# More and smaller products without use in TensorE's early gaps, on an attention and MoE kernel

## The chip, the cores and the metric

The kernel runs on one core of a Trainium2 chip. The metric is the device time of one execution in microseconds (us). Three runs of the kernel before gave 218.28, 218.58 and 218.94 us; their median is 218.58 us. "PE" is TensorE's matmul stream, "PEld" its weight loads, "DVE" VectorE, "ACT" ScalarE, "POOL" GpSimd (which here issues the input transfers) and "SP" SyncE (which issues the stores and the transposing transfers).

## The reference

Inputs are q, k and v of shape (4 batches, 8 heads, 768 positions, 64 channels) and two weights, 512x2048 and 2048x512. In each head every query sees the keys that are less than 16 positions away, and beside them 24 summaries, one for each block of 32 positions: the maximum of the block's keys and the mean of its values.

```python
k_sum = k.reshape(B, H, nb, block, D).max(axis=3)
v_sum = v.reshape(B, H, nb, block, D).mean(axis=3)
# local scores inside the window, and block scores + log(32), in one softmax
a = softmax(concat([where(mask_l, scores_l, -1e9), scores_s + log(block)]))
x = (a @ concat([v, v_sum])).transpose(0, 2, 1, 3).reshape(B * S, H * D)
h = x @ w_in
out = (h * clip(h + 3.0, 0.0, 6.0) / 6.0) @ w_out
```

The attention gives 3072 rows of 512 values, and two dense products with a gate between them make the output of 3072x512 float32.

## The kernel before, in words

Everything is recorded first and issued later. Each piece of work is registered with `plan.op(engine, cost, function, reads, writes, ...)` under a key such as `u03.0`: a letter for the kind, the batch, a number, and after the point the place among the pieces of that kind. The long string ORDER at the top lists all keys in the order in which the planner takes them. `Plan.run` (L141 ff.) gives every piece a begin and an end by fixed costs, gives PSUM banks and buffers to it, and sorts the pieces by begin; each engine then gets its instructions in that order. The planner's times fix nothing but the order and the choice of buffers; on the chip each engine works through its own list and waits on semaphores.

TensorE's pieces near the change are, for batch 0:

- `k0p.0` (`k_step`, L509): 16 transposes of 64x96 blocks of the keys of head pair p into an `h` bank.
- `q0p0.0` (`q_step`, L548): 8 such transposes for the queries.
- `s0p0.0` (`scores`, L629): two products of the identity with a table of large negative numbers, which lay the mask into a score bank; `s0p0.1` (L641) adds the scores themselves, 12 products.
- `u0p.0` (`vsum_first`, L665): 12 products that sum the values by blocks, for head pair p.
- `v00`, `v01`, `v02` (`values` and `finish`, L742 to L746, L775, L779, L797): the weighted sums of the values for 128 rows, their scaling on DVE into a tile `xn`, and four transposes of that by TensorE (L797).
- `q0p1.0` (`q_rest`, L561): three transposes of the rest of the queries.
- `F00...` (`f1`, L815): the first dense product, in parts of 128 columns for the first three groups of features; L820 (ACT) and L822 (DVE) make the gate, and L835 (`f2`) is the second dense product. Pieces `F` and `G` of earlier halves of batches fill TensorE between the attention steps of later ones.
- `u1.0`, `u2.0`, `u3.0` (`vsum`, L682): the sums by blocks for batches 1 to 3, 48 products each. They need every load of that batch's values, among them the short rows that `load_halo` brings (L467, L470).

Input transfers are issued by POOL in ORDER's order: `load_v` (L445), `load_halo` (L467, L470), `load_nat` (L424, L425), `load_raw` (L434), weights (L479, L485). A later transfer on POOL's queue reuses the semaphore of one eight transfers back or so, and waits for its landing.

What the change touches is the last piece of the kernel function. When the order is known, a loop goes over TensorE's pieces in their order and looks at the gap that the planner left ahead of each, up to the planner's time `WARM`. In such a gap it puts products without use: the tile `idle` (all ones) times itself, into a bank that the planner does not use at that time. Before the planner's time SLOW (5.8 us) one product of 512 columns is counted as 0.43, after it as 0.22, with 0.15 of the gap left free:

```python
n = int(max(min(o.begin, SLOW) - end, 0.0) / 0.43 + max(o.begin - 0.15 - max(end, SLOW), 0.0) / 0.22) + (end == BEGIN["PE"])
```

No result reads what these products write, but each one stands in TensorE's list, with a weight load of its own (both at L927), and what follows it on TensorE comes after it.

Of the kernel before, what the change touches and what calls it, by code (L numbers as in the profile page):

```python
# [84 lines left out]
SLOW = 5.8  # L85
# [3 lines left out]
BEGIN = {"PE": 1.6, "ACT": 0.8, "DVE": 0.9, "POOL": 1.4, "SP": 1.0}  # L89
# [138 lines left out]
def kernel(  # L228
# [9 lines left out]
    nc = tc.nc  # L238
    B, H, S, _ = q.shape
# [7 lines left out]
    NTILE = B * 2  # L247
    HQ = NQ // 2
    NS = S // 128
    WARM = 23.0  # L250
    EITHER = ("ACT", "DVE")
    ENGINE = {"DVE": nc.vector, "POOL": nc.gpsimd}
    ET = mybir.EngineType
# [7 lines left out]
    def sb(shape, dt, name):  # L261
        return const.tile(shape, dt, tag=name, name=name)
# [22 lines left out]
    idle = sb([128, 512], BF16, "idle")  # L285
# [635 lines left out]

    def keep(n, o):
        o = o[:, 0] if any(o is x for x in pairs) else o[:]
        for _ in range(n):
            nc.tensor.matmul(o, idle[:, 0:128], idle[:], start=True, stop=True)  # L927

    order = plan.run()
    banks = [s for p in BANKS for _, s in plan.pools[p]]  # L930
    todo, end = [], BEGIN["PE"]
    for o in order:
        if o.eng == "PE" and o.begin < WARM:
            n = int(max(min(o.begin, SLOW) - end, 0.0) / 0.43 + max(o.begin - 0.15 - max(end, SLOW), 0.0) / 0.22) + (end == BEGIN["PE"])
            idle_ = [s for s in banks if not any(a < o.begin and z > end and x is s for a, z, x in plan.lives)]
            if n > 0 and idle_:
                todo.append(lambda n=n, s=idle_[-1]: keep(n, s))
            end = max(end, o.end)
        todo.append(o.fn)
    for fn in todo:  # L940
# [29 lines left out]
```

## Time and profile before

| | |
|---|---|
| runs of the kernel | 218.28, 218.58, 218.94 us, median 218.58 |
| the profiled execution's own time | 219.68 us |
| its span in the profile | 217.9 us, 1.78 us less than its own time |
| PE busy | 207.1 us, 95% of the span |
| DVE, ACT, POOL busy | 148.3, 122.3 and 71.2 us |
| products without use | 19 weight loads of the tile `idle`; 16 of their matmuls are recorded |

The profiled execution is 1.10 us above the median of the three runs. Times in the trace are counted from the start of the span. A row of the timeline merges instructions of one kind that follow each other: start, time from the first start to the last end, engine, line, what is written from what, shapes, count, and in brackets how long the engine stood idle before it and what ended that. Ends of matmuls are modelled and contain the way through the array, so consecutive rows overlap; starts are what one compares. A few matmul records are missing.

### The profile page before, as it was taken

How to read it: one execution, taken by the hardware profiler on the slowest of the kernel's cores; microseconds unless marked ns; L12 is line 12 of the kernel's file. 1: busy time of each engine (PE TensorE's matmuls, PEld its weight loads, DVE VectorE, ACT ScalarE, POOL GpSimd, SP SyncE). 2: the span in 40 equal slices, each digit the busy share in tenths (PEclk: the TensorE clock that was granted, in tenths of full speed). 3: DMA queues.
4: the chain of work that ended last, by engine and by line, in shares of the span. 5: the costliest groups of instructions: out<-in, count | busy, mean ns of one | idle time of the engine just before them, and what ended most of it. 6: DMA issues, size and time to landing. Idle time of an engine off the chain costs nothing.

```text
span 217.9 us, 5201 instructions
## 1 busy us (share of the span) xinstructions
PE 207.1 (95%) x2125; PEld 118.4 (54%) x2151; DVE 148.3 (68%) x304; ACT 122.3 (56%) x236; POOL 71.2 (33%) x90
## 2 busy tenths in 40 slices
PE   7888999999989999989999999999999999999993
PEld 2566666765545555555555555555555555555552
DVE  4878998794898999849987866695555456333301
ACT  5697967797762545777742688833436343423010
POOL 7999369810988466296000000000000000000000
PEclk9999999999999999999999999999999999999999
DMA  5999999999999999999927920005421001201213
GB/s 68 182 156 191 201 164 159 205 195 147 122 120 164 169 122 143 162 172 148 212 52 180 230 26 0 3 0 157 135 48 51 0 2 50 99 0 48 86 59 100
DMA packets 109929, 24.67 MB, mean 113 GB/s; under 512 B 101072, under 2 KB 106960, under 8 KB 109904
## 3 DMA queue, kind: packets, MB, share of 16 engines
q0 software_dynamic: 93440, 14.89, 110.3%
q1 hardware_dynamic: 16464, 9.44, 16.4%
q8 instruction: 17, 0.28, 0.5%
q14 instruction: 8, 0.07, 0.1%
HBM read 29.77 MB, written 6.29 MB: 165 GB/s over the span
## 4 chain that ended last, share of the span: by engine, by line
PE 53%; DMA 25%; POOL 17%; issue 3%; ACT 0%; POOLq 0%; ACTq 0%
PE h L815 23%; PE o L835 22%; DMA vaug<-in_v_dram 20%; DMA win<-in_moe_w_in_dram 5%; PE h L835 5%; POOL nat L434 4%; POOL vaug L445 3%; POOL nat L425 2%; PE S L742 2%; POOL wout L485 1%; PE S L641 1%; POOL qwide L412 1%; POOL win L479 1%; POOL nat L392 1%; POOL nat L399 1%
## 5 line engine op out<-in xcount | busy, mean ns | idle before, releaser
L822 DVE SCALAR_TENSOR_TENSOR g<-r,h 128x384 bf16<-128x384 f32 x128 | 67.8, 547 | 42.6 <-ACT r L820 41.3
L815 PE MATMUL h<-x,win 128*128 128x384 bf16 (+1 forms) x536 | 94.5, 319 | 0.0
L820 ACT ACTIVATE r<-h 128x384 f32<-128x384 f32 x128 | 60.4, 496 | 55.2 <-PE h L815 51.6
L835 PE MATMUL o<-wout,g 128*128 128x512 bf16 x313 | 78.4, 379 | 1.6 <-issue 0.6
L815 PEld LDWEIGHTS <-win 128*128 128x128 bf16 x536 | 49.3, 98 | 34.0 <-issue 0.2
L835 PEld LDWEIGHTS <-g 128*128 128x128 bf16 x400 | 38.2, 98 | 37.2
L651 ACT ACTIVATE at<-S 120x768 bf16<-120x768 f32 x32 | 25.2, 816 | 4.7 <-PE S L641 4.6
L445 POOL DMA_DIRECT2D vaug<-in_v_dram x16 | 15.4, 968 | 4.4 <-DMA wout<-in_moe_w_out_dram 2.3
L655 DVE TENSOR_TENSOR at<-at,mask 96x768 bf16<-96x768 bf16 x28 | 14.7, 550 | 1.7 <-ACT at L651 1.6
L494 ACT COPY ot<-o 128x512 f32<-128x512 f32 x14 | 8.3, 589 | 13.3 <-PE o L835 13.2
L779 DVE TENSOR_TENSOR xn<-S,rc 128x512 bf16<-128x512 f32 x23 | 15.4, 683 | 0.3
L425 POOL DMA_DIRECT2D nat<-in_k_dram x12 | 10.7, 898 | 4.4 <-DMA win<-in_moe_w_in_dram 3.3
L425 POOL DMA_DIRECT2D nat<-in_q_dram x12 | 10.6, 897 | 1.9 <-DMA win<-in_moe_w_in_dram 1.9
L835 PE MATMUL h<-wout,g 128*128 128x256 bf16 (+1 forms) x64 | 10.7, 326 | 0.1
L707 DVE TENSOR_REDUCE red<-kb 128x48 bf16<-128x1536 bf16 x6 | 10.5, 1745 | 0.0
L641 PEld LDWEIGHTS <-kb 64*128 64x128 bf16 x384 | 6.8, 95 | 6.2 <-issue 5.0
L742 PEld LDWEIGHTS <-at 120*64 120x64 bf16 x360 | 6.7, 111 | 4.9 <-issue 2.9
L742 PE MATMUL S<-vaug,at 120*64 120x65 bf16 x352 | 8.0, 197 | 0.9 <-DVE vaug L494 0.9
L494 ACT COPY vaug<-vs 24x768 bf16<-24x768 bf16 x9 | 7.4, 828 | 1.1 <-DVE vs L494 0.9
L494 DVE COPY vaug<-vs 24x768 bf16<-24x768 bf16 x15 | 7.7, 517 | 0.5
L494 ACT COPY ot<-h 128x256 f32<-128x256 f32 (+1 forms) x3 | 1.3, 443 | 11.6 <-PE h L835 11.6
L494 DVE COPY ot<-o 128x512 f32<-128x512 f32 x7 | 4.8, 688 | 4.4 <-PE o L835 2.6
(107 smaller groups left out, 155.8 us busy)
## 6 DMA issues: line engine op xcount, KB each, us to landing
out_dram<-ot SPq DMA_DIRECT2D x19, 256.0 KB, 2.5
vaug<-in_v_dram POOLq DMA_DIRECT2D x16, 192.0 KB, 9.6
win<-in_moe_w_in_dram POOLq DMA_DIRECT2D x4, 512.0 KB, 9.4
wout<-in_moe_w_out_dram POOLq DMA_DIRECT2D x4, 512.0 KB, 10.0
nat<-in_k_dram POOLq DMA_DIRECT2D x12, 128.0 KB, 8.4
nat<-in_q_dram POOLq DMA_DIRECT2D x10, 128.0 KB, 5.4
nat<-in_k_dram POOLq DMA_DIRECT2D x6, 192.0 KB, 6.7
nat<-in_q_dram POOLq DMA_DIRECT2D x6, 192.0 KB, 10.7
```

Of the source, the lines that this page charges most:

```text
L425: nc.gpsimd.dma_start(out=o[n:128], in_=src[b, :, lo + n:lo + 128].rearrange("h r d -> r h d"))
L445: op("POOL", 0.945, lambda: nc.gpsimd.dma_start(out=o[BLK:WIN, lo:hi, 0:D], in_=rows[:, lo:hi]), w=[("v", b % 2, c)], dma=1.28, els=1536)
L494: {"ACT": nc.scalar.copy, "DVE": nc.vector.tensor_copy, "POOL": nc.gpsimd.tensor_copy}[eng](o, i)
L651: op("ACT", 0.81, lambda a=a, x=x: nc.scalar.activation(a, x.slot[0:KEYS, :, 0:HALF], AF.Exp, scale=scl), r=[x], w=[("at", p, half)])
L655: op("DVE", 0.55, lambda m=m, half=half: nc.vector.tensor_tensor(m, m, mask[:, low(half):low(half) + HQ].unsqueeze(1).to_broadcast([WIN, 2 ...
L707: nc.vector.tensor_reduce(red.slot[:].rearrange("x (p u e n) -> x e u p n", p=NP, u=NS, e=2)[:, e], w[:, n * e:n * e + n, BLK:WIN].rearran ...
L742: nc.tensor.matmul(y, a[:, cols], vaug[b % 2][0:KEYS, h, t, 0:D + 1], start=True, stop=True)
L779: nc.vector.tensor_tensor(o, src[..., 0:D], r.unsqueeze(len(r.shape)).to_broadcast(list(o.shape)), op=ALU.mult)
L815: nc.tensor.matmul(h.slot[:, lo * 128:hi * 128], w_in_sb[:, kt, ft * 128:(ft + 1) * 128], xt[s].slot[:, kt, lo * 128:hi * 128], start=(kt ...
L820: op("ACT", 0.49, lambda: nc.scalar.activation(r.slot[:], h.slot[:, 0:HALF], AF.Relu, bias=0.5, scale=1.0 / 6.0), r=[h], w=[r], alloc=r)
L822: op("DVE", 0.553, lambda: nc.vector.scalar_tensor_tensor(gt[s].slot[:, ft], r.slot[:], 1.0, h.slot[:, 0:HALF], op0=ALU.min, op1=ALU.mult) ...
L835: nc.tensor.matmul(o.slot[:, a:z], gt[s].slot[:, ft, ts * 128:(ts + 1) * 128], w_out_sb[:, ft, a:z], start=(ft == 0), stop=(ft == NFT - 1))
```

## The change

The time up to which gaps are looked at, `WARM`, goes from 23.0 to 28.0. Past SLOW, 0.06 of the gap is left free and no longer 0.15, and a 512-column product is counted as 0.2158. What remains of the gap is filled with products of 128 columns (counted as 0.056 each). The part of a gap that lies before SLOW is treated as it was.

```diff
-    WARM = 23.0
+    WARM = 28.0
...
-    def keep(n, o):
+    def keep(n, m, o):
         o = o[:, 0] if any(o is x for x in pairs) else o[:]
-        for _ in range(n):
-            nc.tensor.matmul(o, idle[:, 0:128], idle[:], start=True, stop=True)
+        for c in [512] * n + [128] * m:
+            nc.tensor.matmul(o[:, 0:c], idle[:, 0:128], idle[:, 0:c], start=True, stop=True)
...
         if o.eng == "PE" and o.begin < WARM:
-            n = int(max(min(o.begin, SLOW) - end, 0.0) / 0.43 + max(o.begin - 0.15 - max(end, SLOW), 0.0) / 0.22) + (end == BEGIN["PE"])
+            gap = max(o.begin - 0.06 - max(end, SLOW), 0.0)
+            n = int(max(min(o.begin, SLOW) - end, 0.0) / 0.43) + int(gap / 0.2158) + (end == BEGIN["PE"])
+            m = int(gap % 0.2158 / 0.056)
             idle_ = [s for s in banks if not any(a < o.begin and z > end and x is s for a, z, x in plan.lives)]
-            if n > 0 and idle_:
-                todo.append(lambda n=n, s=idle_[-1]: keep(n, s))
+            if n + m > 0 and idle_:
+                todo.append(lambda n=n, m=m, s=idle_[-1]: keep(n, m, s))
             end = max(end, o.end)
```

In the built program nothing but TensorE's list differs. The products ahead of each piece (a piece that is not named has none, before and after):

| ahead of | before | after | added |
|---|---|---|---|
| `k01.0` (L509) | 9 of 512 | 9 of 512 | none |
| `k03.0` (L509) | 3 of 512 | 4 of 512 | 1 of 512 |
| `s030.0` (L629) | 1 of 512 | 1 of 512, 2 of 128 | 2 of 128 |
| `q010.0` (L548) | 3 of 512 | 3 of 512, 2 of 128 | 2 of 128 |
| `u01.0` (L665) | none | 2 of 128 | 2 of 128 |
| `u03.0` (L665) | 1 of 512 | 1 of 512, 3 of 128 | 3 of 128 |
| `s021.0` (L641) | 2 of 512 | 3 of 512 | 1 of 512 |
| `v02.6` (L797) | none | 1 of 512 | 1 of 512 |
| `F00.10` (L815) | none | 1 of 128 | 1 of 128 |

That is 3 products of 512 columns and 10 of 128 more, each with its weight load: 26 instructions. The new limit `WARM` alone adds none: all pieces in the table begin ahead of the old limit too, and between the old and the new one the planner's list has no gap. New are two waits of such products: the one ahead of `v02.6` writes the `o` bank and waits for DVE's copy out of it (`v00.5`, L494); those ahead of `s021.0` wait for ACT as they did.

## The prediction

> **What bounds the kernel now.** I read the page first: engines, slices, chain.
>
> ```profile
> span 217.9 us, 5201 instructions
> PE 207.1 (95%) x2125; PEld 118.4 (54%) x2151; DVE 148.3 (68%) x304; ACT 122.3 (56%) x236; POOL 71.2 (33%) x90
> ...
> PEclk9999999999999999999999999999999999999999
> ...
> PE 53%; DMA 25%; POOL 17%; issue 3%; ACT 0%; POOLq 0%; ACTq 0%
> ```
>
> TensorE is busy for 95% of the span, at the full granted clock in every slice, yet the chain that ended last holds it for only 53%. The chain in order of time tells where the other part lies:
>
> ```profile
> 18.53 11.76 DMA win<-in_moe_w_in_dram
> ...
> 38.80 15.39 DMA vaug<-in_v_dram
> ...
> 68.05 12.02 DMA vaug<-in_v_dram
> 80.37 11.05 DMA vaug<-in_v_dram
> 91.99 5.00 DMA vaug<-in_v_dram
> 97.03 0.85 PE S L682 x48
> ...
> 204.00 10.14 PE h L835 x60
> ```
>
> Up to 97.03 us it is POOL issuing transfers and transfers landing, with no TensorE piece in it. From 97.03 on it is TensorE, back to back. The timeline shows TensorE's waits between the early stage and there:
>
> ```profile
> 60.30 1.67 PE L835 MATMUL o<-wout,g 128*128 128x512 bf16 x7 [0.16 <-issue]
> 62.84 0.70 PE L742 MATMUL S<-vaug,at 120*64 120x65 bf16 x32 [0.87 <-DVE vaug L494]
> ...
> 95.62 0.85 PE L682 MATMUL S<-vaug,ind 96*32 96x128 bf16 x48
> 97.03 0.85 PE L682 MATMUL S<-vaug,ind 96*32 96x128 bf16 x48 [0.56 <-DMA vaug<-in_v_dram]
> ```
>
> So TensorE comes to `u3.0` 0.56 us before the last transfer of that batch's values has landed. Lateness of TensorE in the first 25 us, if it is carried to here at all, ends here up to 0.56 us. By the same row nothing that only makes TensorE earlier shows at the end.
>
> **The change, part by part.** What a product takes of TensorE once it runs fast, and the early stage itself, from the timeline of PE and of its weight loads:
>
> ```profile
> 1.53 4.02 PE L927 MATMUL o<-idle 128*128 128x512 bf16 x9 [1.53 <-DVE idle L314]
> ...
> 6.04 0.82 PE L927 MATMUL o<-idle 128*128 128x512 bf16 x3
> 7.03 0.87 PE L509 MATMUL h<-ident,nat 96*64 96x96 bf16 x32 [0.17 <-DMA nat<-in_k_dram]
> 8.30 0.48 PE L629 MATMUL S<-bias,ident 128*128 128x384 bf16 x2 [0.40 <-DVE bias L340]
> ...
> 9.01 0.82 PE L927 MATMUL S<-idle 128*128 128x512 bf16 x3
> 9.76 0.36 PE L548 MATMUL h<-ident,nat 96*64 96x96 bf16 x8
> ...
> 15.03 0.50 PE L665 MATMUL o<-vaug,ind 96*32 96x128 bf16 x6
> 16.08 0.49 PE L665 MATMUL o<-vaug,ind 96*32 96x128 bf16 x6 [0.56 <-DVE vaug L494]
> ...
> 17.11 0.84 PE L665 MATMUL h<-vaug,ind 96*32 96x128 bf16 x12 [0.25 <-issue]
> ...
> 20.73 0.38 PE L927 MATMUL h<-idle 128*128 128x512 bf16 x1
> 21.46 0.35 PE L641 MATMUL S<-q,kb 64*128 64x64 bf16 x12 [0.35 <-ACT q L494]
> ...
> 21.92 0.27 PE L797 MATMUL h<-ident,xn 128*128 128x128 bf16 x2
> 22.45 0.28 PE L797 MATMUL h<-ident,xn 128*128 128x128 bf16 x2 [0.25 <-DVE xn L779]
> ...
> 22.79 0.33 PE L561 MATMUL S<-ident,qwide 128*128 128x128 bf16 x3
> 22.96 0.39 PE L815 MATMUL h<-x,win 128*128 128x128 bf16 x4
> ...
> 23.56 1.29 PE L815 MATMUL h<-x,win 128*128 128x128 bf16 x20
> 24.69 0.33 PE L561 MATMUL S<-ident,qwide 128*128 128x128 bf16 x3
> ```
>
> ```profile
> 7.83 0.10 PEld L927 LDWEIGHTS <-idle 128*128 128x128 bf16 x1
> ...
> 9.76 0.23 PEld L548 LDWEIGHTS <-nat 96*64 96x64 bf16 x8 [0.42 <-DMA nat<-in_q_dram]
> ...
> 16.78 0.10 PEld L927 LDWEIGHTS <-idle 128*128 128x128 bf16 x1
> ```
>
> Prices. Three products of 512 columns from 6.04 last 0.82 with 0.38 for the last one (row at 20.73): (0.82 - 0.38) / 2 = 0.22 us from start to start. Twenty products of 128 columns, each with its own load as the added ones have, go from 23.56 to 24.69: 1.13 / 20 = 0.0565 us. The added work is 3 x 0.22 + 10 x 0.0565 = 1.23 us of TensorE's stream, a ceiling if no gap took any of it.
>
> On this price the Trainium skill, "TensorE: Matmul & The Clock Gate", section "Back-to-back issue gap", speaks against the change: a stream of pairs of a load and a 128-column product is given there as about 81 ns a product. By that the ten small ones would take 0.81 us, and the ceiling would be 1.47. The trace disagrees with 56.5 ns for just such pairs, and I go by it.
>
> Now gap by gap, with the start that the added products let through against the start in the row:
>
> - `k03.0`, one of 512: four from 6.04 stream to 6.04 + 0.88 = 6.92; the transposes begin at 7.03, when their keys land. Cost 0; by modelled ends (the wait was 0.17) 0.05.
> - `s030.0`, two of 128: the product whose load stands at 7.83 (its matmul is not recorded), then 0.22 + 0.11, is through at 8.17; DVE's table ends the wait at 8.30. Cost 0 with 0.13 left.
> - `q010.0`, two of 128: 9.01 + 0.66 + 0.11 = 9.78 against 9.76, where the queries land. Cost 0.02; at most the whole 0.11.
> - `u01.0`, two of 128: they push its first six products at 15.03 by 0.11; the next six wait until 16.08 for DVE, idle for 0.56 before. Cost 0.
> - `u03.0`, three of 128: 16.78 + 0.22 + 0.17 = 17.17 against 17.11. What ended the idle 0.25 is named only "issue". If a landing sets 17.11, the cost is 0.06; if the start only follows the product, 0.17.
> - `s021.0`, one of 512: 20.73 + 3 x 0.22 = 21.39 against 21.46, when ACT's copy is done. Cost 0, 0.07 left.
> - `v02.6`, one of 512: 21.92 + 0.22 + two transposes of 0.0565 = 22.25 against 22.45, where the next two wait for DVE's `xn`. Cost 0. Its new wait is for DVE's copy `v00.5`:
>
> ```profile
> 21.10 0.41 DVE L494 COPY x<-o 128x512 bf16<-128x512 bf16 x1
> ```
>
>   That ends at 21.51, before TensorE comes there at 21.92; 0.41 late it would stop `v02.6` and all behind it.
> - `F00.10`, one of 128: no idle time ahead of 22.96, it follows 22.79 at once. Cost 0.06, bare.
> - `WARM`: it adds no product. Cost 0.
>
> The sum when TensorE turns dense near 23 us: 0.02 + 0.06 + 0.06 = 0.14 at the low end, 0.05 + 0.11 + 0.17 + 0.06 = 0.39 at the high end. Does lateness early in the stage survive the waits behind it? The waits at 16.08, 21.46 and 22.45 are for DVE and ACT, which themselves wait for TensorE's results, so I let it through. I take 0.2, nearer the low end, since three of the four rows with a named releaser put the start at a landing or a copy and not at the products.
>
> From there TensorE has no wait worth the name until 62.84, where DVE's copies depend on TensorE's `u1.0`, so I count on no cover there. The 0.56 before 97.03 covers 0.2 and also 0.39. So the path to the end gains nothing: span 217.9 + 0, own time 219.68 + 0. Since that execution stands 1.10 us above the median, I state it on the median: 218.6 us. If the cover is gone (a landing before TensorE comes), the time is 218.58 + 0.14 to 0.39, that is 218.7 to 219.0. A difference of 0.3%, 0.66 us, is about what measurement tells from none here; all of this lies inside it.
>
> **The rivals.**
>
> *The lateness arrives in full.* The 1.10 us by which the profiled execution is longer may be transfers that the profiling slowed, and without it `u3.0` may not wait. Then 218.8, up to 219.0. For it: the wait is just 0.56 and seen in one execution. Against: the chain of landings before it is 12.02, 11.05 and 5.00 us long, so the queue is full there.
>
> *The products close gaps that are already closed (slower).* In timed runs the early landings and copies may come earlier against TensorE than in the profile; `k03.0`, `q010.0`, `u03.0` and `s021.0` have 0.13 us or less to spare here. Every product then stands bare in TensorE's list, and DVE and ACT, which wait for these pieces, slip too. The price goes up to the ceiling 1.23: 219.8 without the cover at 97.03, 218.58 + 1.23 - 0.56 = 219.25 with it. It decides against me once lateness at 97.03 is over 0.66 without the cover, or 1.22 with it. Products issued before the fast stage cost more: the nine from 1.53 take 4.02, with 0.63 for the last, (4.02 - 0.63) / 8 = 0.42 each:
>
> ```profile
> L927 PE MATMUL o<-idle x12: 379/634/634, 1.5 to 6.5; 128*128 128x512 bf16 x12
> ```
>
> So an execution whose fast stage begins later pays double for the one ahead of `k03.0`.
>
> *The products keep the clock up (faster).* If in timed runs TensorE falls back to the slow rate in the early gaps, filling them prevents it. Such a spell, as long as the slow start here (4.02 us) and at about half the pace (0.42 against 0.22), would cost up to 2.0 us, of which the wait at 97.03 hides 0.56; winning back the other 1.4 gives 218.58 - 1.4 = 217.2, and less the more of it the waits of the early stage hid. Against it: the products at 9.01 and 23.56 run at full pace after gaps of up to 0.56, and the three runs lie within 0.66 us.
>
> The Trainium skill, same page, section "Why this matters for your kernels", has the fall back to half rate only after idle gaps over about 3.4 us; by that the rival gives no gain at all, 218.6. The trace agrees as far as it goes: no idle time behind 1.53 is longer than 0.87.
>
> *The change does nothing.* That the later limit adds nothing is plain from the list; that the products do nothing for the clock is my forecast. It gives 218.6 too.
>
> **How the numbers follow.** No gain, and lateness covered at 97.03: 0.46, 218.6. Lateness arrives in full: 0.20, 218.8 to 219.0. Slower beyond 0.66: 0.20, 219.25 to 219.8. Faster beyond 0.66: 0.14, 217.2 to 217.9. The first two are "within 0.3%": 0.66. The likeliest gives 218.6, its own range 218.2 to 219.0 (the spread of the three runs and the high end of the lateness). The range that leaves out no more than 2 in 10 reaches into both other cases: 217.8 to 219.5.
>
> **What would show it.** 32 loads of `idle` on PE, ten of their products with 128 columns; the start of the dense stage at L815 (22.96) later by 0.1 to 0.4; the waits at 7.03 and 8.30 shorter by up to 0.17 and 0.11, those at 21.46 and 22.45 by about 0.2; the wait at 97.03 shorter by what L815 is later, and its start unchanged; the stretch from 97 to the end as long as now. I am wrong if L682 at 97.03 starts later with no wait for a transfer, if a new wait stands at L927 or L797, or if products behind 6 us run at 0.42 in one of the kernels.

## The result, and the profile after

The changed kernel takes 219.83 us (median of 19 runs, 219.02 to 220.96); the kernel before took 218.85 us in 19 runs beside it. The ratio is 1.0041, with a 95% interval of 1.0022 to 1.0061: slower by 0.9 us, between 0.5 and 1.3. I had forecast 218.6 and no change, with a range up to 219.5.

The page of the changed kernel: span, busy time of the engines, chain by engine.

```profile
span 218.0 us, 5253 instructions
...
PE 210.1 (96%) x2164; PEld 119.1 (55%) x2164; DVE 146.3 (67%) x304; ACT 122.5 (56%) x236; POOL 71.1 (33%) x90
...
PE 88%; DVE 5%; DMA 3%; issue 1%; ACT 1%; POOL 0%; DVEq 0%; ACTq 0%; POOLq 0%
```

The span is nearly that of before (217.9), since the execution profiled before was longer than most of its kernel (219.68 against the median of 218.85). So the two spans say nothing; the chain does. It held TensorE for 53% and now holds it for 88%: behind the landing of the keys at 7.75 us no transfer stands in it up to 97 us any more. The timeline of PE in this kernel, early stage, around the last sums by blocks, and near 164 us:

```profile
5.57 1.04 PE L927 MATMUL o<-idle 128*128 128x512 bf16 x4
7.79 0.87 PE L509 MATMUL h<-ident,nat 96*64 96x96 bf16 x32 [1.18 <-DMA nat<-in_k_dram]
...
10.51 0.36 PE L548 MATMUL h<-ident,nat 96*64 96x96 bf16 x8
...
16.84 0.49 PE L665 MATMUL o<-vaug,ind 96*32 96x128 bf16 x6 [0.25 <-DVE vaug L494]
...
18.04 0.84 PE L665 MATMUL h<-vaug,ind 96*32 96x128 bf16 x12
...
23.68 0.33 PE L561 MATMUL S<-ident,qwide 128*128 128x128 bf16 x3
...
23.91 0.39 PE L815 MATMUL h<-x,win 128*128 128x128 bf16 x4
...
95.94 1.52 PE L682 MATMUL S<-vaug,ind 96*32 96x128 bf16 x96
...
162.71 1.03 PE L835 MATMUL o<-wout,g 128*128 128x512 bf16 x4
164.10 2.11 PE L815 MATMUL h<-x,win 128*128 128x384 bf16 x12 [0.36 <-DVE g L822]
```

Two things stand out. `u2.0` and `u3.0` (95.94) run through as one group of 96, with no wait: the cover is gone. And a wait stands at 164.10, where the kernel before had none, as its own timeline shows:

```profile
163.13 1.03 PE L835 MATMUL o<-wout,g 128*128 128x512 bf16 x4
163.99 2.11 PE L815 MATMUL h<-x,win 128*128 128x384 bf16 x12
```

From the start of the four products at L835 to the next L815 it is 0.86 us before and 1.39 after: 0.53 us lost at a place 140 us behind the last added product. It is not won back: from the L815 that follows `u3.0` (97.82 before, 97.39 after) to the end of the span it is 120.1 us before and 120.6 after. (The wait is put down to DVE; the transfer that ended it comes below.)

### The profile page after: what moved, and what is told of

Its sections match the earlier page's. It is cut to its first block, busy times and chain, and to the rows that moved or that the text cites. A ratio compares the mean times of both kernels' runs of the same rounds, so it can differ in the third digit from the quotient of the medians.

```text
span 218.0 us, 5253 instructions
## 1 busy us (share of the span) xinstructions
PE 210.1 (96%) x2164; PEld 119.1 (55%) x2164; DVE 146.3 (67%) x304; ACT 122.5 (56%) x236; POOL 71.1 (33%) x90
## 4 chain that ended last, share of the span: by engine, by line
PE 88%; DVE 5%; DMA 3%; issue 1%; ACT 1%; POOL 0%; DVEq 0%; ACTq 0%; POOLq 0%
PE h L815 38%; PE o L835 33%; PE h L835 5%; PE S L742 3%; PE S L641 3%; DMA nat<-in_k_dram 3%; DVE vaug L494 2%; PE S L592 1%; PE S L682 1%; DVE xn L779 1%; PE S L797 1%; PE h L665 1%; DVE g L822 0%; PE h L509 0%; PE S L927 0%
## 5 line engine op out<-in xcount | busy, mean ns | idle before, releaser
L815 PE MATMUL h<-x,win 128*128 128x384 bf16 (+1 forms) x536 | 94.5, 319 | 0.5 <-DVE g L822 0.4
L835 PE MATMUL o<-wout,g 128*128 128x512 bf16 x336 | 81.4, 379 | 0.0
L815 PEld LDWEIGHTS <-win 128*128 128x128 bf16 x536 | 49.3, 98 | 34.7 <-issue 1.0
L835 PEld LDWEIGHTS <-g 128*128 128x128 bf16 x400 | 38.2, 98 | 37.2
L494 ACT COPY ot<-o 128x512 f32<-128x512 f32 x14 | 8.3, 590 | 12.5 <-PE o L835 12.4
L835 PE MATMUL h<-wout,g 128*128 128x256 bf16 (+1 forms) x64 | 10.7, 326 | 0.0
L641 PEld LDWEIGHTS <-kb 64*128 64x128 bf16 x384 | 6.7, 95 | 6.0 <-issue 5.0
L494 ACT COPY vaug<-vs 24x768 bf16<-24x768 bf16 x9 | 7.5, 828 | 1.1 <-DVE vs L494 0.9
L494 ACT COPY ot<-h 128x256 f32<-128x256 f32 (+1 forms) x3 | 1.3, 443 | 11.6 <-PE h L835 11.6
L494 DVE COPY ot<-o 128x512 f32<-128x512 f32 x7 | 4.8, 686 | 4.1 <-PE o L835 4.1
L927 PE MATMUL o<-idle 128*128 128x512 bf16 (+1 forms) x19 | 5.6, 430 | 1.5 <-DVE idle L314 1.5
```

Source lines behind the costliest of these rows:

```text
L494: {"ACT": nc.scalar.copy, "DVE": nc.vector.tensor_copy, "POOL": nc.gpsimd.tensor_copy}[eng](o, i)
L641: nc.tensor.matmul(X[p, half].slot[:, j, i * QB:(i + 1) * QB], keys, asks, start=not masked, stop=not masked or i == HQ - 1)
L815: nc.tensor.matmul(h.slot[:, lo * 128:hi * 128], w_in_sb[:, kt, ft * 128:(ft + 1) * 128], xt[s].slot[:, kt, lo * 128:hi * 128], start=(kt ...
L835: nc.tensor.matmul(o.slot[:, a:z], gt[s].slot[:, ft, ts * 128:(ts + 1) * 128], w_out_sb[:, ft, a:z], start=(ft == 0), stop=(ft == NFT - 1))
```

## The experiments

Theory A is the prediction's: the wait near 97 us covers the early lateness. Theory B: that wait belonged to one execution, and lateness counts in full.

**The kernel before again, and the change in three parts.** In `e1_early`, `e2_mid` and `e3_late` the new count holds only for the pieces named; all others keep the old formula. The diff is `e1_early`'s; `e2_mid` names `u01.0` and `u03.0`, `e3_late` `s021.0`, `v02.6` and `F00.10`.

```diff
+            if o.key not in ('k03.0', 's030.0', 'q010.0'):
+                n = int(max(min(o.begin, SLOW) - end, 0.0) / 0.43 + max(o.begin - 0.15 - max(end, SLOW), 0.0) / 0.22) + (end == BEGIN["PE"])
+                m = 0
```

> The kernel before, unchanged, as a measure of how far two equal kernels come apart here and of how often TensorE waits for the last transfer of batch 3's values. Ratio 1.000, within 0.002. Theory A (the wait of 0.56 us at L682 near 97 us stands in most executions and covers lateness): the wait is there again, 0.3 us or more. Theory B (the wait was one execution's; usually TensorE is the later one and lateness counts in full): no wait at L682 near 97 us, and the chain is TensorE's from the early stage on.

> Only the products added ahead of k03.0, s030.0 and q010.0: one of 512 columns and four of 128. Theory A: 0.0 us. Theory B with the gaps as the prediction read them: +0.02 to 0.16 us. Theory C (the added products stand bare, since in most executions the work is ready when TensorE comes): up to 0.22 + 4 x 0.0565 = +0.45 us.

> Only the products added ahead of u01.0 and u03.0: five of 128 columns. Theory A: 0.0 us. Theory B: +0.06 to 0.17 us, all from u03.0. Theory C: +0.28 us.

> Only the products added ahead of s021.0, v02.6 and F00.10: two of 512 columns and one of 128. Theory A: 0.0 us. Theory B: +0.06 us, the bare one ahead of F00.10. Theory C: up to 2 x 0.22 + 0.0565 = +0.50 us. If the new wait of the product ahead of v02.6 for DVE's copy is what costs, it shows as idle time at L927, and this kernel alone is as slow as the whole change.

| kernel | ratio to before, 95% interval | median us (before 218.82) |
|---|---|---|
| e0_again | 1.0027, 0.9996 to 1.0058 | 218.91 |
| e1_early | 1.0000, 0.9971 to 1.0030 | 219.12 |
| e2_mid | 1.0012, 0.9979 to 1.0044 | 219.33 |
| e3_late | 0.9986, 0.9958 to 1.0013 | 218.75 |

No part alone is measurably slower, but the intervals are 0.6 us to either side, too wide to tell theory A from B. (The equal kernel came out 0.27% away, more than the 0.2% that I had expected.) The traces tell more. The timeline of PE in the kernel before, taken again:

```profile
7.25 0.87 PE L509 MATMUL h<-ident,nat 96*64 96x96 bf16 x32 [0.38 <-DMA nat<-in_k_dram]
8.05 0.39 PE L927 MATMUL o<-idle 128*128 128x512 bf16 x1
8.28 0.49 PE L629 MATMUL S<-bias,ident 128*128 128x384 bf16 x2
...
9.77 0.36 PE L548 MATMUL h<-ident,nat 96*64 96x96 bf16 x8
...
16.12 0.49 PE L665 MATMUL o<-vaug,ind 96*32 96x128 bf16 x6 [0.59 <-DVE vaug L494]
...
17.15 0.84 PE L665 MATMUL h<-vaug,ind 96*32 96x128 bf16 x12
...
26.42 0.81 PE L815 MATMUL h<-x,win 128*128 128x384 bf16 x4 [0.43 <-DVE g L822]
...
95.31 1.66 PE L682 MATMUL S<-vaug,ind 96*32 96x128 bf16 x96
```

The same kernel has no wait near 97 us here. Of all fourteen traces two have it: the first one of the kernel before, and that of `f1_count` below (0.67 us, in an execution of 222.28 us, its slowest). The keys of `k03.0` landed at 7.25 and not at 7.03, and `s030.0` at 8.28 follows the product at 8.05 at once, where the first profile showed an idle 0.40 (the product whose matmul is not recorded lies in it). So two covers that the prediction counted on are not there in every execution. And there is one that it did not have: TensorE waits for DVE ahead of 26.42. None of the three parts shows a wait near 164 us.

**A known dose.** Eight products of 512 columns were put into the dense stage near 24 us of the kernel before.

```diff
+            if o.key == "F00.15":
+                n = 8
```

> The kernel before with eight products of 512 columns, 8 x 0.2158 = 1.73 us, put into the dense stage near 24 us, where TensorE has no gap. Theory A (the wait near 97 us covers 0.56 us): +1.17 us. Theory B: +1.7 us, with L682 near 97 us later by 1.7 and no wait there. If DVE and ACT had slack that gives some back: less than 1.2.

Measured: 1.0080 (1.0050 to 1.0110), that is +1.75 us (1.1 to 2.4); L682 ran through as one group at 96.43. The time does not tell the theories apart, since theory A's 1.17 lies inside the interval too. What speaks against theory A is that the wait near 97 us is missing in twelve of fourteen traces. Nor did L682 move by the 1.7 of theory B: against the kernel before, taken again, it is 1.12 later. The wait ahead of 26.42 took up 0.5 of the dose: the L815 group in front of it moved from 24.89 to 26.59, the one behind it from 26.42 to 27.62. So how much of an early lateness arrives can differ from execution to execution.

**Fewer products.** `e4_none` has only the start-up products; `e7_trim` is the kernel before, with its old count, without those ahead of three pieces (the second edit).

```diff
+            if o.key != "k01.0":
+                n = m = 0
...
+            if o.key in ("s030.0", "q010.0", "u03.0"):
+                n = 0
```

> No products without use behind k01.0 at all: the ten of 512 columns of the kernel before are left out too. Theory B alone (products cost where they stand bare): those ahead of s030.0, q010.0 and u03.0 stand bare in the trace of the kernel before taken again, so 0.22 to 1.1 us faster. Theory E (the products hold the clock up): the clock falls to 0.5 for a window of 3.4 us in many executions, as it did once in e2_mid, and the time is 0.5 to 2 us longer.

> The kernel before without its five products ahead of s030.0, q010.0 and u03.0; those ahead of k03.0 and s021.0, which wait for a landing and for ACT, stay. Theory B: 0.2 us (u03.0) to 0.5 us faster, and never slower. Theory E: slower, with windows of the clock at 0.5 behind k03.0.

`e4_none` is slower: 1.0137 (1.0095 to 1.0180). Its profile by stretches: length, then busy time of PE, PEld, DVE, ACT and POOL, granted clock, DMA share and GB/s.

```profile
4.30:7.60 3.30, 1.61 (x37) 0.88 (x37) 1.44 (x3) 0.92 (x4) 3.08 (x8) 1.00 1.19 172
7.80:17.80 10.00, 9.53 (x127) 6.20 (x123) 6.94 (x14) 7.66 (x17) 9.86 (x14) 0.50 2.16 165
18.00:24.60 6.60, 5.10 (x131) 4.17 (x128) 5.72 (x18) 4.13 (x9) 4.72 (x8) 1.00 1.25 206
24.90:28.10 3.20, 3.19 (x38) 2.64 (x37) 2.90 (x8) 2.71 (x5) 0.84 (x2) 0.50 1.55 189
```

The clock falls to half for 10.2 us and once more for 3.4 by the trace's record of the clock, and all six executions had a mean granted clock of 0.992 or less. So the products do hold the clock; theory E is right about their use. But the ones that the kernel before has are enough in nearly all executions: of 102 executions of it, two had a mean granted clock below 0.9935 (half the clock for 3.4 of 218 us makes it 0.992); of 38 of the changed kernel none had. `e7_trim` measured 1.0007 (0.9981 to 1.0033), with such spells in two of 12 executions. What the bare products cost and what they save may cancel out there; no run isolates it.

**Where the rest comes from.** The whole change was run again:

> The whole change again, beside the following kernels on one chip. Theory B (no wait at L682 near 97 us in most executions, so lateness of the early stage counts in full): from the segments of the traces so far the products cost 0.20 between k03.0 and q010.0 and 0.17 ahead of u03.0 and 0.02 to 0.06 behind v00, so +0.4 us wherever the keys of k03.0 land as they do in the kernel before. Theory D (beyond that, the whole change also makes those keys land later): +0.9 us, with k03.0 starting at 7.7 or later behind a wait for a transfer; without D k03.0 starts between 7.0 and 7.4 when that wait ends it.

It gave 1.0064 (1.0042 to 1.0086), +1.4 us, although `k03.0` began at 7.25: theory D (later keys) falls. The parts cannot explain it either. But the wait near 164 us was there again, and in none of the eight traces of other kernels so far. What differs there is a transfer. In the whole change, the window from the start of the second of two transposing transfers (`x<-xn`, L789, issued by SP for the last half batch) shows:

```profile
DMA packets 544, 0.13 MB, mean 55 GB/s; under 512 B 544, under 2 KB 544, under 8 KB 544
q1 hardware_dynamic: 544, 0.13, 73.1%
x<-xn SPq DMA_TRANSPOSE x1, 3.8
```

and the same window in the kernel before, taken again:

```profile
DMA packets 544, 0.13 MB, mean 55 GB/s; under 512 B 544, under 2 KB 544, under 8 KB 544
q1 hardware_dynamic: 544, 0.13, 27.2%
x<-xn SPq DMA_TRANSPOSE x1, 2.5
```

The same 544 packets of the same bytes take 73.1% of 16 engines' window against 27.2%, and land 3.8 us behind their issue, not 2.5. In the changed kernel the last transfer of this kind is issued at 160.2:

```profile
L789 SPq DMA_TRANSPOSE x<-xn x12: 1190/1221/1975, 110.1 to 160.2; - x12
```

160.2 + 3.8 = 164.0, and L815 starts at 164.10. In `e6_whole` the profile itself names this transfer as what ended the wait:

```profile
164.96 2.11 PE L815 MATMUL h<-x,win 128*128 128x384 bf16 x12 [0.51 <-DMA x<-xn]
```

What else moves at that moment is one transfer of 16,384 bytes on the instruction queue (q8). Such blocks come through the whole run; the trace's records of transfers put this one at 161.31 us in the changed kernel and at 164.28 and 163.40 in the two traces of the kernel before. If the block holds TensorE's instructions, 26 added ones bring its end 26 instructions forward in TensorE's work; at 12 pairs of load and product in 1.95 us (L815) I estimate that as 2.1 us. The block's 1.16 us from 161.31 overlap the packets of the second transposing transfer, which run from 161.45 to 163.35. That is theory F.

The Trainium skill, "Runtime: NRT & Kernel Launch", section "Instruction fetch mechanics", says that a sequencer refills its instructions in blocks of 16 KiB by a DMA queue of its own, at a cost that is mostly hidden. The trace agrees with the size. No wait of TensorE stands at the block where it lies apart from the transfer (`f3_merged`, at 163.2); where they meet the cost is not hidden.

Three new kernels test it, beside the whole change once more. `f1_count` adds 26 instructions and no time in a gap; `f2_more` gives the whole change 36 further instructions; `f3_merged` gives every gap the whole change's columns with fewer instructions. The loop in `keep` reads, in this order:

```diff
+        for c in [512] * (n - 5) + [128] * 16 + [256] * 2 if n == 9 else [512] * n:
...
+        for c in [512] * (n - 6) + [128] * 24 if n == 9 else [512] * n + [128] * m:
...
+        for c in [512] * n + [128 * m] * (m > 0):
```

> The kernel before with five of the nine 512-column products of the start-up cut into smaller ones of the same columns in sum (16 of 128 and 2 of 256), so that TensorE's list has 26 instructions more, as many as the whole change adds, and no work in any later gap. Theory F (the 26 instructions move a 16 KB transfer of instructions from about 163.4 to 160.8 us, onto the second of two transposing transfers, whose 0.87 us become 1.9 to 2.0, and TensorE waits at L815 near 164 us): a wait of 0.3 to 0.6 us there, and +0.5 to 0.7 us. Theory B alone (only the lateness of the early stage): 0.0 us and no such wait.

> The whole change with six of the nine start-up products cut into four of 128 columns each: 36 instructions more than the whole change, no work more. The transfer of instructions should then lie near 157 us, ahead of both transposing transfers. Theory F: no wait at L815 near 164 us, and +0.4 us against the kernel before (the early lateness alone), unless another transfer of instructions now meets another transposing one. Theory B alone: as slow as the whole change beside it.

> The whole change with the 128-column products of one gap joined to one product of 256 or 384 columns: the same columns in every gap, but 16 instructions more than the kernel before and not 26. The transfer of instructions should lie near 161.8 us, when the second transposing transfer is just through. Theory F: at most 0.1 us of wait near 164 us, and +0.4 us. Theory B alone: as slow as the whole change beside it.

> The whole change once more, on the same chip as the three above. Theory F: the wait of 0.3 to 0.6 us at L815 near 164 us is there for the third time, and the time is +0.9 to 1.1 us: 0.4 of early lateness and 0.5 to 0.7 of the wait. Theory B alone: +0.4 us.

| kernel | instructions added to TensorE | ratio, 95% interval | block on q8, us behind the issue of the two transfers | second transfer, us | L835 to L815 near 164, us |
|---|---|---|---|---|---|
| before, e0_again | 0 | 1 | 4.90, 4.92 | 0.88, 0.88 | 0.86, 0.86 |
| whole change, e6_whole, e8_whole | 26 | 1.0041, 1.0064, 1.0040 | 2.35, 2.41, 3.00 | 1.90, 2.03, 2.28 | 1.39, 1.53, 1.75 |
| f1_count | 26 | 1.0034, 1.0007 to 1.0061 | 2.49 | 2.15 | 1.63 |
| f2_more | 62 | 1.0023, 0.9998 to 1.0047 | -0.99 | 0.88 | 0.87 |
| f3_merged | 16 | 1.0000, 0.9977 to 1.0023 | 4.93 | 0.88 | 0.86 |

(For e8_whole the interval is 1.0018 to 1.0062. The second transfer starts 2.5 us behind the issue.) All four traces whose block starts in or just ahead of the second transfer have it stretched, and all have the wait; the ten others (those in the table without it, and e1_early, e2_mid, e3_late, e4_none, e5_dose and e7_trim, with blocks 4.7 to 7.4 us behind the issue) have neither. From the L815 that follows `u3.0` to the end of the span it is 120.6 to 121.0 us in the four, and 119.9 to 120.1 in nine of the ten (120.4 in `e4_none`). `f1_count` is the decisive one: its timeline near 166 us, with no product added in any gap,

```profile
165.03 1.03 PE L835 MATMUL o<-wout,g 128*128 128x512 bf16 x4
166.66 1.62 PE L815 MATMUL h<-x,win 128*128 128x384 bf16 x9 [0.60 <-DMA x<-xn]
```

and its transfers in the window of the second transfer:

```profile
q1 hardware_dynamic: 544, 0.13, 75.8%
q8 instruction: 1, 0.02, 3.4%
```

against `f3_merged`, which does all the added work:

```profile
162.06 1.03 PE L835 MATMUL o<-wout,g 128*128 128x512 bf16 x4
162.92 2.11 PE L815 MATMUL h<-x,win 128*128 128x384 bf16 x12
```

```profile
q1 hardware_dynamic: 544, 0.13, 27.5%
x<-xn SPq DMA_TRANSPOSE x1, 2.5
```

Theory B alone expected the opposite for both. On one chip the whole change's median was 219.88 us and `f3_merged`'s 219.27. The time of `f2_more` lies between the two and decides nothing; its trace fits theory F. It does not follow that `f1_count` owes all of its +0.7 us to this wait: 1.63 - 0.86 = 0.77 fits, but the interval runs from 0.15 to 1.3 us.

Where the block comes to lie was forecast less well. In `f2_more` it starts at 158.3 and not near 157. In `f3_merged` it starts at 163.2 and not near 161.8: with 16 instructions more it lies where the kernel before has it, as it nearly does with 6, 10 and 16 in `e3_late`, `e1_early`, `e2_mid` and `e5_dose` (4.7 to 5.0 behind the issue). It moved by 1.9 to 2.6 us with 26. So the shift does not follow the count in proportion; what sets its steps stays open.

## Why the prediction was wrong, point by point

- **The sum of "The change, part by part" lacked a term: the step that failed.** It counted the 26 instructions by the time that their products take, and "the path to the end gains nothing" followed from that. It left out that they can shift the program against its own instruction blocks. That term measured 0.53, 0.67, 0.89 and 0.77 us in four traces (the last column less 0.86), the larger part of the +0.9. It shows in the sign "the stretch from 97 to the end as long as now", which became 0.5 to 0.9 us longer.
- **"The 0.56 before 97.03 covers 0.2 and also 0.39": fell.** In the kernel before, taken again, the wait was not there, nor in the profile after. I read one execution's wait as the kernel's. The rival "the lateness arrives in full", at 0.20, was right that this cover can be missing; that the lateness arrives in full is not shown. That there is no cover between 23 and 62.84 does not hold in every execution either: the wait of 0.43 ahead of 26.42 is one.
- **The gap-by-gap sum held in size.** From the start of `k03.0` to L815 it is 15.93 and 15.75 us in the two traces of before, and 16.12, 16.11 and 15.96 in the three of the whole change: about 0.2 us more, where I had 0.14 to 0.39. In detail: ahead of `u03.0` (from the second half of `u01.0`) 1.03 became 18.04 - 16.84 = 1.20, so the 0.17 of the high end and not 0.06: the start followed the products. From `k03.0` to `q010.0`, 9.77 - 7.25 = 2.52 became 10.51 - 7.79 = 2.72: the 0.20 that I had at 0.02, since the spare 0.13 ahead of `s030.0` was gone with the later keys. (With the earlier keys of the first profile the waits made it 2.73.) `F00.10` took 0.23 behind 23.68, before 0.17: the bare 0.06, as said. `u01.0`, `s021.0` and `v02.6` cost nothing, as said, and no wait stood at L927 for DVE's copy. This count starts at `k03.0` and leaves out the product ahead of it, which I had at 0 to 0.05. In `e1_early`, where full speed began only at 7.2 us, the four products there took 1.41 us, 0.35 each, and `k03.0` followed them at 7.68 with no wait for its keys.
- **How much of those 0.2 reaches the end stays open.** `f3_merged`, with all the lateness and without the collision, measured 1.0000, or 0.5 us to either side. Between 24 and 97 us single executions come apart by more than that: the wait at 62.84 in the first profile, for one. L682 began at 95.29 in `f3_merged` and at 95.22 in `e8_whole`, no later than the 95.31 and 95.62 in the two traces of before.
- **The price of a 128-column product held** for eight of the ten added ones: by segments they cost what 0.0565 us each makes, not the 81 ns that the prediction quotes from the Trainium skill. The two ahead of `u01.0` made their segment 0.3 us longer, which the wait for DVE behind it hid.
- **The rival "the products keep the clock up"** had the right mechanism and no room: `e4_none` shows the fall, but the kernel before already prevents nearly all of it. The Trainium skill's rule of idle gaps, by which I gave no gain (the section that I named says over about 3 us, another place on that page 3.4), is contradicted by `e4_none`, where the clock fell behind idle times of at most 1.57 us.

```profile
7.21 1.10 PE L509 MATMUL h<-ident,nat 96*64 96x96 bf16 x32 [1.57 <-DMA nat<-in_k_dram]
```

- **"Slower beyond 0.66" had 0.20** and a mechanism (all products bare, up to 1.23) that did not happen. The sign was right for a reason that the prediction does not name.

## What to carry to other kernels

An edit that adds or removes instructions can move later instruction blocks of that engine; where a block meets a transfer that the engine will soon wait for, the time changes far from the edit. Look through the trace for new waits behind the place of the edit, and for what the instruction queue moves just then. Two tests tell such a wait from the cost of the work: the same number of instructions without the work, and the same work in fewer instructions. The second was also the cure here, with some luck, since its block did not come where I expected it. And a wait that is to cover a cost has to be seen in more than one execution.

## What the runs showed of the hardware that I had not expected

- One 16,384-byte block on the instruction queue (0.93 to 1.31 us by its own record in the four traces) stretched a 544-packet transposing transfer from 0.88 to between 1.90 and 2.28 us. In the stretched part the transfer trickles at 4 to 13 GB/s where it ran at about 200. By the trace's records 13 to 15 of its 544 packets take over 1 us there and all others under 0.1; in the unstretched transfers none takes over 0.06. That looks as if one of the 16 DMA engines still held its share while the others waited. The Trainium skill, "DMA: Bandwidth & Descriptors", section "Queues, rings and completion order", has each engine switch between queues only after whole packets; a large packet of the instruction queue ahead of many small ones on one engine would look like this. That it is this, no run isolates.
- The clock fell to half behind a stretch in which PE was busy for 1.61 of 3.30 us (`e4_none`, 4.30 to 7.60), and in the profile of `e2_mid` after the keys of `k03.0` landed late and TensorE had stood idle for 1.74 us. In the changed kernel a stretch with 2.16 of 3.30 us busy held it. Busy time alone is no threshold: in `e4_none` the clock fell again behind 18.00 to 24.60 with 5.10 of 6.60 us busy.
